# Smaller first loads, earlier loads for the third batch, and closer transposes in a fused attention and rational feed-forward kernel

## Chip, cores and metric

The kernel runs on one core of one Trainium2 chip. The metric is the device time of one execution in microseconds (us). The experiments ran in three jobs, each on one core of a chip of its own (chip 14 for e1 to e4, 6 for e5 to e8, 9 for e9 to e12), and each job also timed the kernel before beside its own kernels; so times are compared within a job, and between jobs only as ratios to the kernel before. For a single core a run counts as slow when it is over 1.5% above the fastest run of the same kernel; one run here was (it is named below), and it is left out of the ratios.

## The reference

Eight batches of attention over 12 heads, 448 tokens and 64 channels per head, with one extra unit in the softmax's denominator; then a feed-forward layer whose activation is a quotient of two polynomials.

```python
scores = scale * q @ k.T                      # batch 8, heads 12, seq 448, head_dim 64
e      = exp(scores - m)
attn   = e / (sum(e) + exp(-m) + 1e-9)
x      = (attn @ v) as [8 * 448, 768]
h      = x @ w_in                             # [768, 2048]
g      = (a0 + a1*h + a2*h^2 + a3*h^3) / (1 + |b0|*|h| + |b1|*h^2 + 1e-6)
out    = g @ w_out                            # [2048, 768], float32
```

## The kernel before

The kernel is a software pipeline over batches. In slot `n` (six slots to a batch) it makes the scores and exponentials of one pair of heads, while the feed-forward layer of the batch before (`gemm1`, product with `w_in`) and of the one before that (`gemm2`, product with `w_out`) fill TensorE. A list of (slot, function) is sorted by slot; TensorE and ScalarE follow that order exactly. VectorE, GpSimd and SyncE are placed by a scheduler, so for them the slot only sets the order in which work is offered.

The loads go out from GpSimd. Batches 0 and 1 have q and k transposed on TensorE (`transpose_pair`); from batch 2 on a DMA transposes them (`transpose_dma`), issued from SyncE.

```python
    def load(b, quads=range(NQ)):
        if quads[0] == 0:
            ...                                   # tiles q4, k4, v4, qT, kT of this batch; zero two margins of q4
        for qd in quads:                          # four heads at a time, 224 KB per tensor
            h0, h1 = 4 * qd, 4 * qd + 4
            nc.gpsimd.dma_start(out=k4[:, h0*w:h1*w]..., in_=runs(k))
            nc.gpsimd.dma_start(out=q4[:, D+h0*w:D+h1*w]..., in_=runs(q))
            nc.gpsimd.dma_start(out=v4[:, h0:h1]..., in_=runs(v))

    def transpose_dma(b):
        nc.sync.dma_start_transpose(out=kT..., in_=k4)                       # kT
        nc.sync.dma_start_transpose(out=qT[:, T:]...[:, :, 0, :], in_=q4[:, D:D + H*NJ*D])
        nc.sync.dma_start_transpose(out=qT[:, 0:2*nb*T]...[:, :, 0, :], in_=q4[:, 0:H*NJ*D])
        nc.sync.dma_start_transpose(out=qT[:, 2*nb*T:]..., in_=q4[:, H*NJ*D:])

    def transpose_pair(b, p):
        g0, g1 = 8 * p + (1 if p else 0), 8 * p + 9      # pair 0: nine blocks of q, the ninth reads head 2
        for i, g in enumerate(range(g0, g1)):
            nc.tensor.transpose(tq[...], q4[:, g * D:(g + 2) * D], ident[0:T, 0:T])
        nc.vector.tensor_copy(out=qT[...], in_=tq[...])
        ...                                              # four blocks of k, the same way, into kT

    load(0, [0])
    ...
    load_w_in(0, 2); load(1, [0]); load_w_in(1, 2); load(1, range(1, NQ))

    for b in range(B):
        if b >= 2:
            work.append((b * NP - NP - 1.5, load, (b,)))
            work.append((b * NP - NP - 1.49, transpose_dma, (b,)))
        for p in range(NP):
            n = b * NP + p
            if b < 2:
                work.append((n - 0.95, transpose_pair, (b, p)))
            ...                                          # scores at n + 0.0 and n + 0.5
        for qd in range(NQ):
            n = b * NP + 2 * qd
            work.append((n + 2.02, sums, (b, qd)))
            work.append((n + 2.52, attend, (b, qd)))
        ...                                              # gemm1, the activation, gemm2
    work.append((2 * NP - NP - 1.4, load_w_out, ()))     # 3 MB in one DMA
```

The softmax here doesn't subtract the row's maximum and nothing guards it: scores larger than these inputs give would overflow.

## Time and profile before

| | |
|---|---|
| time | 470.21 us, median of 3 (469.68 to 471.07) |
| span of the profiled run | 468.7 us |
| TensorE / VectorE / ScalarE busy | 93% / 78% / 65% |

The table of stretches gives busy time per engine in a stretch of time. The columns are: stretch and its length, then busy time and count of instructions of PE (TensorE matmuls), PEld (weight loads), DVE (VectorE), ACT (ScalarE) and POOL (GpSimd), then granted TensorE clock (1.00 is full speed, 0.50 half), mean busy share of the DMA engines, and GB/s. In the lines of this document `sps` are scores, `e` their exponentials, `den` and `rden` the sums and their reciprocals, `u` the product with v, `hp` the product with `w_in`, `op` that with `w_out`; `tq` and `tk` are transposes on TensorE.

```profile
core 0: us, PE busy (x) PEld busy (x) DVE busy (x) ACT busy (x) POOL busy (x), PEclk, DMA share, GB/s
...
70.00:80.00 10.00, 6.00 (x39) 2.15 (x37) 7.84 (x12) 5.92 (x7) 2.40 (x6) 0.79 0.83 137
80.00:90.00 10.00, 10.00 (x76) 4.09 (x73) 7.19 (x12) 8.54 (x9) 9.15 (x15) 0.87 1.37 181
90.00:100.00 10.00, 7.06 (x66) 2.75 (x64) 9.15 (x13) 7.58 (x9) 1.33 (x2) 0.82 1.39 185
...
200.00:300.00 100.00, 99.82 (x771) 48.61 (x770) 87.36 (x126) 69.69 (x73) 9.03 (x17) 1.00 0.55 92
```

From 200 to 300 us TensorE is full at full clock. In the stretches from 70 to 100 us it has holes (times in which TensorE idles), and the clock is down. The list of waits between 60 and 105 us says what for (engine, line, whom it waited for; total us, times, longest):

```profile
PE sps L178 <- DMA qT<-q: 3.7, 1, 3.7
PE sps L178 <- ACT e L183: 3.6, 4, 2.5
```

The chain of waits is followed back from the last instruction. Its early part, in order of time (start, length, what):

```profile
6.04 7.71 DMA k<-in_k_dram
...
14.03 12.95 DMA q<-in_q_dram
...
27.27 11.84 DMA v<-in_v_dram
...
39.40 9.15 DMA k<-in_k_dram
...
48.64 15.27 SPq L100
...
64.02 5.91 SPq L102
...
69.99 7.44 DMA qT<-q
77.43 0.14 issue
77.56 0.99 PE sps L178 x4
```

All that stands before the third batch's scores at 77.56 us is transfers: the loads, and then the DMA transposes, which take 29 us from 48.6 us on. qT comes in three pieces, the last of them short; I call the landing of the second piece (the third of the four DMA transposes), at 77.43 us, the gate. GpSimd's own timeline shows what shares the DMA engines with the transposes (start, length, engine, line, operation, what ended the idle time before it):

```profile
41.80 1.17 POOL L164 DMA_DIRECT2D w_out_sb<-in_moe_w_out_dram  x1 [0.46 <-DMA q<-in_q_dram]
70.32 0.72 POOL L85 DMA_DIRECT2D k<-in_k_dram  x1 [27.36 <-DMA kT<-k]
77.76 0.15 POOL L68 MEMSET q<- 112x64 f16 x1 [6.72 <-DMA qT<-q]
...
79.95 2.10 POOL L90 DMA_DIRECT2D v<-in_v_dram  x3 [0.29 <-issue]
```

`w_out` goes out before the transposes start. The third batch's v goes out after the gate, because GpSimd, which works in order, first waits for qT at a memset.

### The profile page before, as it was taken

To read this page: it belongs to the slowest core of one execution; us is meant where nothing else is said; L and a number is where in the kernel's file an instruction comes from. 1 tells how busy PE (TensorE), PEld (TensorE's weight loads), DVE (VectorE), ACT (ScalarE), POOL (GpSimd) and SP (SyncE) were. 2 spreads that over 40 slices of the span, in tenths; PEclk is the share of its full clock that TensorE was granted. 3 is DMA by queue.
4 is the path that set the end of the run, shared out by engine and by line. 5 is a ranking of instruction groups with operands and counts; after the bars stand their busy time and mean duration, and the time that the engine had idled before them with its cause. 6 is when DMAs were issued, how large, how long until landed. Compare 5 with 4: busy or idle time off the path is not lost.

```text
span 468.7 us, 8030 instructions
## 1 busy us (share of the span) xinstructions
PE 436.7 (93%) x3346; PEld 214.3 (46%) x3346; DVE 364.6 (78%) x536; ACT 307.0 (65%) x331; POOL 76.8 (16%) x133
## 2 busy tenths in 40 slices
PE   2888986979999999999999999999999999999695
PEld 1444432434444454444544444444444445555353
DVE  1234796988999988888989998888989989999800
ACT  2788686667778675659588766658686773566411
POOL 7443003713314001230020001010000000200000
PEclk9999997979999999999999999999999999999989
DMA  9999998999798418991391109811011100110222
GB/s 123 205 205 196 206 169 135 191 180 175 132 167 152 73 31 144 166 149 36 66 184 60 35 0 169 138 34 36 1 34 35 35 23 12 40 48 16 67 69 67
DMA packets 91764, 46.90 MB, mean 100 GB/s; under 512 B 52304, under 2 KB 86608, under 8 KB 91728
## 3 DMA queue, kind: packets, MB, share of 16 engines
q0 software_dynamic: 37136, 22.81, 34.7%
q1 hardware_dynamic: 54592, 23.58, 26.0%
q8 instruction: 26, 0.43, 0.4%
q14 instruction: 10, 0.08, 0.1%
HBM read 45.62 MB, written 11.01 MB: 121 GB/s over the span
## 4 chain that ended last, share of the span: by engine, by line
PE 69%; DMA 10%; DVE 7%; ACT 5%; SPq 5%; issue 1%; POOL 1%; DVEq 0%; POOLq 0%
PE op L322 28%; PE hp L224 24%; PE sps L178 7%; PE u L189 7%; ACT e L183 4%; DMA k<-in_k_dram 4%; PE den L189 4%; SPq L100 3%; DMA q<-in_q_dram 3%; DMA v<-in_v_dram 3%; DMA qT<-q 2%; SPq L102 1%; DVE w L268 1%; DVE g L284 1%; DVE w L273 1%
## 5 line engine op out<-in xcount | busy, mean ns | idle before, releaser
L183 ACT ACTIVATE e<-sps 112x896 f16<-112x896 f32 x192 | 164.6, 915 | 103.8 <-PE sps L178 103.7
L224 PE MATMUL hp<-xt,w_in_sb 128*128 128x448 f16 x768 | 163.4, 357 | 0.6 <-ACT rden L201 0.6
L322 PE MATMUL op<-w_out_sb,g 128*128 128x384 f16 x768 | 133.4, 329 | 3.7 <-DVE g L284 3.7
L224 PEld LDWEIGHTS <-w_in_sb 128*128 128x128 f16 x768 | 68.9, 98 | 84.6 <-issue 31.3
L322 PEld LDWEIGHTS <-g 128*128 128x128 f16 x768 | 75.5, 99 | 57.1 <-DVE g L284 4.4
L232 DVE CAST g<-hp 128x448 f16<-128x448 f32 x112 | 69.1, 619 | 21.0 <-PE hp L224 20.9
L178 PE MATMUL sps<-qT,kT 64*112 64x448 f16 x384 | 64.2, 390 | 15.1 <-ACT e L183 8.7
L279 ACT ACTIVATE c<-c,oneeps_c 128x1792 f16<-128x1792 f16 (+1 forms) x33 | 57.4, 1740 | 14.9 <-DVE c L261 14.9
L283 ACT ACTIVATE c<-c 128x1792 f16<-128x1792 f16 (+1 forms) x33 | 54.5, 1650 | 0.1
L298 POOL COPY gx<-g 128x256 f16<-128x256 f16 x32 | 16.6, 533 | 194.1 <-DVE g L284 131.1
L178 PEld LDWEIGHTS <-kT 64*112 64x112 f16 x384 | 21.1, 129 | 53.0 <-issue 48.5
L284 DVE TENSOR_TENSOR g<-w,c 128x1792 f16<-128x1792 f16 (+1 forms) x33 | 35.5, 1075 | 12.5 <-ACT c L283 12.0
L189 PE MATMUL u<-e,v 112*32 112x448 f16 x768 | 43.0, 368 | 0.0
L261 DVE TENSOR_TENSOR c<-c,w 128x1792 f16<-128x1792 f16 (+1 forms) x33 | 35.1, 1063 | 0.9
L273 DVE TENSOR_TENSOR w<-w,g 128x1792 f16<-128x1792 f16 (+1 forms) x33 | 35.0, 1059 | 0.4
L268 DVE TENSOR_TENSOR w<-w,g 128x1792 f16<-128x1792 f16 (+1 forms) x33 | 34.9, 1056 | 0.4
L213 DVE TENSOR_TENSOR xt<-u,rden 128x448 f16<-128x448 f32 x48 | 29.1, 618 | 6.3 <-PE u L189 6.0
L329 DVE COPY osb<-op 128x384 f32<-128x384 f32 x48 | 26.5, 552 | 5.7 <-PE op L322 5.2
L85 POOL DMA_DIRECT2D k<-in_k_dram x24 | 17.4, 727 | 80.4 <-DMA kT<-k 74.9
L189 PEld LDWEIGHTS <-v 112*32 112x32 f16 x768 | 18.9, 99 | 21.7 <-issue 9.3
L121 DVE COPY qT<-tq 128x896 f16<-128x896 f16 (+1 forms) x12 | 7.6, 632 | 22.9 <-PE tq L119 22.9
L90 POOL DMA_DIRECT2D v<-in_v_dram x24 | 17.5, 732 | 45.0 <-PE u L189 41.8
(37 smaller groups left out, 278.7 us busy)
## 6 DMA issues: line engine op xcount, KB each, us to landing
k<-in_k_dram POOLq DMA_DIRECT2D x24, 224.0 KB, 8.3
q<-in_q_dram POOLq DMA_DIRECT2D x24, 224.0 KB, 7.5
v<-in_v_dram POOLq DMA_DIRECT2D x24, 224.0 KB, 7.4
w_in_sb<-in_moe_w_in_dram POOLq DMA_DIRECT2D x8, 384.0 KB, 12.7
w_out_sb<-in_moe_w_out_dram POOLq DMA_DIRECT2D x1, 3072.0 KB, 26.0
out_dram<-osb SPq DMA_DIRECT2D x8, 336.0 KB, 2.7
out_dram<-osb SPq DMA_DIRECT2D x8, 288.0 KB, 3.1
out_dram<-osb SPq DMA_DIRECT2D x8, 240.0 KB, 2.6
```

The lines of the kernel that those rows point to most:

```text
L178: nc.tensor.matmul(out=sps[0:T, half, 0:S], lhsT=kT[r, (2 * h + i) * T:(2 * h + i + 1) * T], rhs=qT[r, c:c + S], start=True, stop=True,)
L183: nc.scalar.activation(out=e, in_=sps[0:T, :, 0:S], func=AF.Exp, scale=scale)
L189: nc.tensor.matmul(out=dst[32 * t:32 * t + 32, 0:S], lhsT=w(4 * qd + t, j), rhs=ets[b, 4 * qd + t, j // 2][:, j % 2, :], start=(j == 0), s ...
L224: nc.tensor.matmul(out=hp[:, 0:S], lhsT=w_in_sb[:, c, fc * 128:(fc + 1) * 128], rhs=xt[:, c, :], start=(c == 0), stop=(c == NDC - 1),)
L232: nc.vector.tensor_copy(out=h, in_=hp[:, 0:S])
L261: nc.vector.tensor_tensor(out=c, in0=c, in1=ns[b, gi, f0], op=ALU.mult)
L268: nc.vector.tensor_tensor(out=m, in0=m, in1=h, op=ALU.mult)
L273: nc.vector.tensor_tensor(out=m, in0=m, in1=h, op=ALU.mult)
L279: nc.scalar.activation(out=c, in_=c, func=AF.Ln, bias=oneeps_c)
L283: nc.scalar.activation(out=c, in_=c, func=AF.Exp, scale=-1.0)
L284: nc.vector.tensor_tensor(out=gs[b, gi][:, f0:f0 + n, :], in0=ns.pop((b, gi, f0)), in1=c, op=ALU.mult)
L322: nc.tensor.matmul(out=op[:, 0:HD], lhsT=lhs(fc), rhs=w_out_sb[:, fc, nh * HD:(nh + 1) * HD], start=(fc == 0), stop=(fc == NFC - 1),)
```

## The change

Its intent is to start sooner (first loads by two heads, so that the first transposes needn't wait for four), to bring the third batch's q and k in sooner, and to place transposes closer to the scores that need them. The core of the diff:

```diff
-    load(0, [0])
+    load(0, "kq", [0], 0, 2)
+    load(0, "kq", [0], 2, 4)
...
-    for qd in range(1, NQ):
-        load(0, [qd])
+    load(0, "v", [0])
+    load(0, "kqv", range(1, NQ))
...
     load_w_in(0, 2)
-    load(1, [0])
+    load(1, "kq", [0])
     load_w_in(1, 2)
-    load(1, range(1, NQ))
+    load(1, "v", [0])
+    load(1, "kqv", range(1, NQ))
...
         if b >= 2:
-            work.append((b * NP - NP - 1.5, load, (b,)))
-            work.append((b * NP - NP - 1.49, transpose_dma, (b,)))
+            n = b * NP - NP - (3.5 if b == 2 else 1.5)
+            work.append((n, load, (b, "kq")))
+            work.append((n + 0.01, transpose_dma, (b,)))
+            work.append((n + 0.02, load, (b, "v")))
...
-                work.append((n - 0.95, transpose_pair, (b, p)))
+                early = (0.75, 0.6)[b] if n else 1
+                work.append((n - early, transpose_pair, (b, p)))
...
-            work.append((n + 2.52, attend, (b, qd)))
+            work.append((n + (2.52 if b else 2.3), attend, (b, qd)))
...
-    work.append((2 * NP - NP - 1.4, load_w_out, ()))
+    work.append((NP - 3.4, load_w_out, ()))
```

`load` now takes which tensors and which heads of a quad to load; with all of them it issues what it issued before.

More of the change, by code (lines that the diff above doesn't have):

```diff
@@ L62, with tiles_of, load @@
     loaded = {}
-    def load(b, quads=range(NQ)):
-        if quads[0] == 0:
-            q4 = ld.tile([T, D + H * NJ * D + D], F16, tag="q4", name="q4")
-            eng = nc.vector if b == 0 else nc.gpsimd
-            eng.memset(q4[:, 0:D], 0.0)
-            eng.memset(q4[:, D + H * NJ * D:], 0.0)
-            loaded[b] = (
-                q4,
-                ld.tile([T, H * NJ * D], F16, tag="k4", name="k4"),
-                ld.tile([T, H, NJ, D], F16, tag="v4", name="v4", bufs=2),
-                ld.tile([128, (1 + H * NJ) * T], F16, tag="qT", name="qT", bufs=2),
-                ld.tile([128, H * NJ // 2 * T], F16, tag="kT", name="kT", bufs=2),
-            )
+    def tiles_of(b):
+        q4 = ld.tile([T, D + H * NJ * D + D], F16, tag="q4", name="q4")
+        eng = nc.vector if b == 0 else nc.gpsimd
+        eng.memset(q4[:, 0:D], 0.0)
+        eng.memset(q4[:, D + H * NJ * D:], 0.0)
+        loaded[b] = (
+            q4,
+            ld.tile([T, H * NJ * D], F16, tag="k4", name="k4"),
+            ld.tile([T, H, NJ, D], F16, tag="v4", name="v4", bufs=2),
+            ld.tile([128, (1 + H * NJ) * T], F16, tag="qT", name="qT", bufs=2),
+            ld.tile([128, H * NJ // 2 * T], F16, tag="kT", name="kT", bufs=2),
+        )
+    def load(b, what, quads=range(NQ), t0=0, t1=4):
+        if b not in loaded:
+            tiles_of(b)
         q4, k4, v4, _, _ = loaded[b]
@@ L80, in load @@
         for qd in quads:
-            def runs(src):
-                return src[b].rearrange("(t g) (p j) d -> g p t (j d)", g=NQ, j=NJ)[qd]
-            h0, h1 = 4 * qd, 4 * qd + 4
-            nc.gpsimd.dma_start(
-                out=k4[:, h0 * w:h1 * w].rearrange("p (h x) -> p h x", x=w), in_=runs(k))
-            nc.gpsimd.dma_start(
-                out=q4[:, D + h0 * w:D + h1 * w].rearrange("p (h x) -> p h x", x=w),
-                in_=runs(q))
-            nc.gpsimd.dma_start(
-                out=v4[:, h0:h1].rearrange("p h j d -> p h (j d)"), in_=runs(v))
+            h0, h1 = 4 * qd + t0, 4 * qd + t1
+            for one in what:
+                src, dst = {
+                    "k": (k, k4[:, h0 * w:h1 * w].rearrange("p (h x) -> p h x", x=w)),
+                    "q": (q, q4[:, D + h0 * w:D + h1 * w].rearrange(
+                        "p (h x) -> p h x", x=w)),
+                    "v": (v, v4[:, h0:h1].rearrange("p h j d -> p h (j d)")),
+                }[one]
+                nc.gpsimd.dma_start(out=dst, in_=src[b].rearrange(
+                    "(t g) (p j) d -> g p t (j d)", g=NQ, j=NJ)[qd, :, t0:t1])
     def transpose_dma(b):
```

## The prediction

> **What bounds it now.** By the table of stretches, TensorE is busy 99 to 100% at full clock from 110 to 440 us: that work is conserved. Before it there are holes. TensorE waits 7.0 us for the first queries; then scores and exponentials take turns until about 40 us. The weightiest hole is at 73.8 to 77.56 us: the list of waits gives "scores, for the DMA of qT", 3.7 us, and the chain of waits runs back from it through transfers alone to the first load. So the third batch's DMA transposes, landed at 77.43 us, are a gate: what TensorE gains before 74 us only widens the hole. The granted clock falls to 0.50 at about 76 to 83 us, and again at 96 to 103 us, after a 2.5 us hole that waits for ScalarE behind VectorE. (The Trainium skill, "TensorE: Matmul & The Clock Gate", Part 1, gives windows of 3.4 us; both half-clock stretches last 6.8 us, which agrees.)
>
> **What the change does, read from the built order of instructions.**
> 1. First loads by two heads. The first transposes can start about 1.2 us sooner, but the ninth transpose of pair 0 reads head 2, which comes with the second half, at about 7.0 us again. Eight are then done: first scores some 0.7 us sooner (9.11 to about 8.4, an estimate from 0.11 us per cold transpose). The stream of transfers is full either way (about 200 GB/s from 4 to 64 us).
> 2. Transposes later by 0.2 to 0.35 of a slot, first batch's attend sooner: swaps of neighbours, no work added. Up to 2 us sooner before the gate, nothing after it.
> 3. Third batch's loads. GpSimd's order is nearly the old one: the same bytes stand ahead of its q and k, and w_out still follows them. So k lands near 48.5 us and the transposes still share the queues with w_out. The trace's packet records show about 112 packets a microsecond of each while both run, and up to 1000 for transposes alone: alternation by packet, as the Trainium skill says ("DMA: Bandwidth & Descriptors", Queues, rings and completion order). The one real move: the three v loads (224 KB each) issue right behind the fourth batch's first k, near 71 us, not at 80 us after qT has landed. They meet the tail of the qT transposes: some 290 more packets of 60 ns alternate with it on 16 engines, an estimated 1 us later at most, 0.5 us in the middle. v is needed at 97 us and was no wait before.
>
> **On the critical path.** Earlier start of the stream, -0.2 us; contention with v, +0.5 us; half-clock stretches in other windows, -1 us with luck. The gains of 1 and 2 are swallowed by the gate.
>
> **Prediction: 469.6 us, 466.5 to 472.2 us.** Faster by over 2%: 0.03; within 2%: 0.95; slower by over 2%: 0.02.
>
> **What the profile would show.** First scores at about 8.4 us. The hole before the third batch's scores still there and wider (4 to 6 us), ended by the DMA of qT at 76.5 to 79 us. v landed before 85 us. The hole near 94 us of about 2.5 us still there. From 110 us on, the same length within 1 us.
>
> **What would make it wrong.** If qT lands several microseconds sooner, because q and k of batch 2 or w_out are issued sooner than I think, the clock stays full, and 5 to 8 us are to be had. If v takes its full share for all its 3.4 us, the gate moves by 3 us: 473 us or more. If the second half-clock stretch vanishes, 3 us are gained that I don't count on.

## The result

The changed kernel took 470.99 us in the median (470.33 to 471.46, 4 runs); the kernel before, timed beside it, took 470.48 us (469.68 to 471.07, 4 runs). The ratio is 1.0011, with a 95% interval of 0.9991 to 1.0031. Ratios here are the mean time of one kernel's fast runs over that of the other's of the same rounds, so they aren't quite the ratio of the medians. In a later job (run e11) the ratio was 1.0072 (0.9991 to 1.0154). So the change does nothing that can be told from zero.

The profile after, however, is not that of before. The stretches:

```profile
70.00:80.00 10.00, 8.40 (x75) 3.75 (x72) 10.00 (x17) 8.09 (x9) 2.95 (x4) 1.00 1.42 135
80.00:90.00 10.00, 8.46 (x82) 3.59 (x81) 9.73 (x15) 8.59 (x10) 7.72 (x13) 1.00 1.23 153
90.00:100.00 10.00, 7.27 (x68) 3.14 (x69) 9.89 (x15) 7.79 (x10) 2.27 (x4) 0.99 1.39 188
...
200.00:300.00 100.00, 99.82 (x773) 48.70 (x770) 87.40 (x126) 70.16 (x74) 9.50 (x17) 1.00 0.55 92
```

The clock is full where it was down. The same waits between 60 and 105 us:

```profile
PE sps L176 <- ACT e L181: 4.4, 5, 2.2
...
PE sps L176 <- DMA qT<-q: 1.3, 1, 1.3
```

The hole before the third batch's scores shrank from 3.7 to 1.3 us. But the chain shows that the gate did not come sooner; it came 4.0 us later (81.41 us for 77.43 us):

```profile
49.20 15.59 SPq L97
...
64.90 4.65 SPq L99
...
69.60 11.81 DMA qT<-q
81.41 0.14 issue
81.55 0.59 PE sps L176 x4
```

The hole shrank because TensorE itself came later. GpSimd's timeline shows v in its new place, before the wait for qT:

```profile
69.89 0.72 POOL L91 DMA_DIRECT2D k<-in_k_dram  x1 [26.06 <-DMA kT<-k]
70.60 2.35 POOL L91 DMA_DIRECT2D v<-in_v_dram  x3
82.28 0.49 POOL L67 MEMSET q<- 112x64 f16 x1 [9.33 <-DMA qT<-q]
```

Reading four marks off the two traces accounts for the whole result:

| us | before | after | difference |
|---|---|---|---|
| TensorE done with all it may do before the third batch's scores ("arrival") | 73.82 | 80.23 | +6.4 |
| third batch's scores start | 77.56 | 81.55 | +4.0 |
| first product with `w_out` starts | 104.07 | 104.53 | +0.5 |
| from there to the end | 364.6 | 364.6 | 0.0 |

TensorE is 6.4 us later, and the gate is 4.0 us later. From the gate to the first product with `w_out`, before needed 26.5 us, of which 12.0 us were at half clock by the clock records (75.9 to 82.7 us and 96.3 to 103.2 us, counted from the gate on); after needs 23.0 us with 3.4 us at half clock. That is 3.5 us won back. That it goes with the clock is borne out by all 14 profiles: this stretch takes 21.3 to 22.7 us with no half clock in it (five profiles), 23.0 to 24.0 us with 3.4 us of it (four, and 25.1 us in e6, which also waits for v), 25.8 and 26.0 us with 10.2 us, and 26.5 and 27.2 us with 12.0 and 12.6 us. The last row (span minus third row) shows that nothing behind that point matters: it lies between 364.3 and 364.7 us in every profile, so the rest of this document is about the first 105 us.

### The profile page after: what moved, and what is told of

Read it like the earlier page. It is cut to its first block, busy times and chain, and to the rows that moved or that the text cites. A ratio compares the mean times of both kernels' runs of the same rounds, so it can differ in the third digit from the quotient of the medians.

```text
span 469.2 us, 8033 instructions
## 1 busy us (share of the span) xinstructions
PE 436.0 (93%) x3346; PEld 215.1 (46%) x3346; DVE 364.5 (78%) x536; ACT 306.9 (65%) x331; POOL 78.8 (17%) x135
## 4 chain that ended last, share of the span: by engine, by line
PE 68%; DMA 11%; DVE 7%; ACT 5%; SPq 4%; issue 1%; POOL 1%; DVEq 0%; POOLq 0%
PE op L320 28%; PE hp L222 23%; PE sps L176 7%; PE u L187 7%; ACT e L181 4%; DMA k<-in_k_dram 4%; PE den L187 3%; SPq L97 3%; DMA q<-in_q_dram 3%; DMA v<-in_v_dram 3%; DMA qT<-q 3%; SPq L99 1%; DVE w L266 1%; DVE g L282 1%; DVE w L271 1%
## 5 line engine op out<-in xcount | busy, mean ns | idle before, releaser
L327 DVE COPY osb<-op 128x384 f32<-128x384 f32 x48 | 26.5, 552 | 5.7 <-PE op L320 5.5
L252 DVE TENSOR_SCALAR c<-w,babs 128x1792 f16<-128x1792 f16 (+1 forms) x33 | 24.5, 741 | 0.2
```

## The experiments

### What the parts do to the built program

Before any run, each part of the change was built alone. The third batch's part (the slots of its loads and of `w_out`) leaves the instruction lists of all five engines, with their waits, unchanged (but for the numbers in buffers' names): put into the kernel before, it gives the program of before; taken out of the changed kernel, it gives the changed program. The scheduler places these loads by when their buffers come free, and the slot did not decide. What moves the third batch's v ahead of the wait for qT is the placing of the transposes and of the attend together; each alone leaves v behind it. So three parts remain to be run.

Theory A, after reading the traces: the attend, moved in front of the second pair of scores, starves ScalarE and delays TensorE by about 6 us; the early v delays the gate; the two delays meet at the gate, hide each other, and spare the half clock. The rivals: B, the first loads or the transposes cause the late arrival; C, the gate is late for a reason other than v.

The first job ran e1 to e4, five rounds each, sharing 11 runs of the kernel before: median 470.58 us, but from 465.98 to 471.81 us. That scatter is far wider than in the first three runs (469.68 to 471.07), and it limits what times can say; the marks in the profiles are sharper.

### e1: the attend alone

```diff
-            work.append((n + 2.52, attend, (b, qd)))
+            work.append((n + (2.52 if b else 2.3), attend, (b, qd)))
```

> Only the first batch's attend is moved from slot 2.52 to 2.3; the order on VectorE and ScalarE is that of before, and the third batch's v stays behind qT. Theory A (the attend in front of the second pair of scores starves ScalarE): TensorE comes to the third batch's scores 3 to 6 us later than before's 73.8 us, at 77 to 80 us; the hole before them shrinks from 3.7 us to under 1 us; qT still lands at 77 to 78 us; time 466 to 470 us, because the half-clock stretch behind the hole goes too. Rival B (the late arrival in the changed kernel comes from its first loads and from the half-clock stretch they set off): TensorE comes within 1.5 us of 73.8 us, the hole stays over 2.5 us, time as before within 0.7 us.

It took 468.78 us (467.35 to 469.55), ratio 0.9982 (0.9939 to 1.0026). TensorE's timeline at the gate:

```profile
76.47 2.44 PE L220 MATMUL hp<-xt,w_in_sb 128*128 128x448 f16 x12
78.85 0.89 PE L174 MATMUL sps<-qT,kT 64*112 64x448 f16 x4
```

The arrival is at 78.92 us, 5.1 us later than before, qT landed at 76.69 us (a little sooner than expected), and there is no wait and no half clock behind it. Theory A holds and rival B fails as the main cause. Slower before the gate turned out no slower at the end.

### e2: the transposes alone

```diff
-                work.append((n - 0.95, transpose_pair, (b, p)))
+                early = (0.75, 0.6)[b] if n else 1
+                work.append((n - early, transpose_pair, (b, p)))
```

> Only the transposes of the first two batches are placed closer (0.75 and 0.6 instead of 0.95). Theory A: little of the late arrival is theirs; TensorE comes to the gate within 2 us of before's 73.8 us, the hole stays 2 to 5 us, qT lands at 77 to 78 us, time as before within 1 us. Rival (the placement of the transposes is what delays TensorE, since scores then wait for the copies of qT and kT): arrival at 77 us or later, hole under 1 us.

It took 469.84 us (466.03 to 471.02), ratio 1.0000 (0.9951 to 1.0049). The arrival is at 75.82 us, the hole 2.4 us, qT landed at 78.07 us. This is as theory A expected, at its edge: in this one profile the arrival is 2.0 us later, with 6.8 us of half clock before the gate that the first profile of before has not.

### e3: the first loads alone

```diff
-    load(0, "kqv", [0])
+    load(0, "kq", [0], 0, 2)
+    load(0, "kq", [0], 2, 4)
...                                # and batch 1's first v behind the second half of w_in
```

> Only the first loads are cut to two heads and the second batch's first v goes behind the second half of w_in. The first transposes start near 5.8 us, the ninth near 8.2 us, the first scores near 9.6 us instead of 9.1 us (as in the changed kernel). Theory A: that half a microsecond is swallowed by the gate, qT lands at 77 to 78.5 us, the hole is 2.5 to 4 us, time as before within 1 us. Rival B (the first loads set the late arrival of the changed kernel): arrival at 77 us or later.

It took 470.81 us in the median of all six runs (465.54 to 472.98); the ratio is 1.0026 (0.9970 to 1.0082), with the one slow run (472.98 us) left out. Its profile fell on a quick execution (465.54 us): no half clock behind the gate. The ninth transpose of q ran at 7.66 us and the first scores at 9.00 us, not at the expected 9.6 us. The arrival is at 76.85 us, which misses theory A's hole of 2.5 us (1.0 us) and comes close to B's 77 us; this profile has two half-clock stretches before the gate, which the first profile of before has not. So on e3 alone the first loads aren't cleared; e12 decides.

### e4: the changed kernel with v held back

```diff
+    def v_after_qT(b):
+        v4, qT = loaded[b][2:4]
+        x = H * NJ * T - 3
+        nc.gpsimd.tensor_copy(out=v4[:, 0:H:4, 0, 0:2],
+                              in_=qT[0:T, x:x + 2 * NQ].rearrange("p (a c) -> p a c", c=2))
...
+            if b == 2:
+                work.append((n + 0.015, v_after_qT, (b,)))
             work.append((n + 0.02, load, (b, "v")))
```

The copied elements are overwritten by the load; the copy is there only so that the load has to wait for qT.

> The changed kernel with one thing added: the third batch's three v loads wait for its qT, as they did before, through a six-element copy per partition on GpSimd; the orders on TensorE, ScalarE and VectorE are those of the changed kernel. Theory A (v's packets alternate with those of the transposes and delay the gate): qT lands at 77 to 79 us instead of 81.4 us; TensorE, which arrives at about 80.2 us, waits for it no more; time 1 to 2 us under the changed kernel, 469 to 470 us. Rival C (the gate is late because VectorE is busy throughout or the transposes stall by themselves, not because of v): qT lands at 80.5 us or later, time within 0.5 us of the changed kernel's 471.0 us.

It took 469.88 us (468.79 to 470.49), ratio 1.0006 (0.9964 to 1.0049). qT landed at 80.61 us, only 0.8 us sooner than in the changed kernel. On this number rival C wins: v alone is not what made the gate late, and 0.8 us is no more than two executions of one kernel differ by (e8). The time falls where theory A had put it, but it comes from another job than the changed kernel's 470.99 us, and its ratio to before tells nothing.

### e5: the changed kernel with v and the next k held back

This is e4, with the same kind of copy in front of the fourth batch's first k, so that no load at all meets the last two transposes.

> The changed kernel with the third batch's v and the fourth batch's first k both held back until the third batch's qT has landed, so that no load shares the queues with its last two transposes. The orders on TensorE, ScalarE and VectorE stay those of the changed kernel. With v alone held back (e4) qT landed at 80.61 us, against 81.41 us in the changed kernel and 77.43 us before. Theory D (any load whose packets trickle in beside the transposes slows them, and e4 still had one): qT lands at 75 to 78 us, TensorE, arriving near 80.3 us, no longer waits; time as e4, 468.5 to 470.5 us. Rival E (the transposes are late by themselves in this order: the transfers start about 1.1 us later, and a 16 KB instruction fetch near 70.7 us falls into the second transpose): qT lands at 79 us or later all the same.

The second piece of qT landed at 77.28 us (the short third at 78.29 us), and TensorE, arriving at 79.64 us, waited for nothing. In this order theory D holds, E fails. It took 468.94 us (467.39 to 470.24), ratio 0.9966 (0.9928 to 1.0003). So in the changed order the loads beside the transposes cost 4.1 us at the gate (81.41 less 77.28, from two jobs); taking v away first gives back 0.8 us of it, and the rest goes when k is held back too. k alone was not held back. D is no general rule, though: before had the same k beside its transposes and landed at 77.43 us.

Why k costs more in the changed order is open. Two differences between the traces suggest themselves: the stream of loads runs about 1.1 us later (by the packet records it passes 2016 KB at 16.0 us for 14.9 us), and VectorE is busy without a break at 70 to 80 us (10.00 of 10 us, for 7.84 before). Other runs speak against both. e3 has the same k beside its transposes, its loads as late (its first DMA transpose goes out at 49.14 us, that of the changed kernel at 49.20 us), and VectorE busy for the same 10.00 us; its qT landed at 77.75 us. e12 has the late loads (49.34 us) and landed at 78.82 us; e1 has the busy VectorE (10.00 us) and landed at 76.69 us. v landed 11.4 us after its issue in the changed kernel (median), queued behind k and beside the transposes, and 6.2 us before, where VectorE was idle; but it took 5.3 us in e1 and 5.2 us in e4, with VectorE busy throughout. The Trainium skill ("SBUF — State Buffer", the box on DMAs issued from GpSimd under "SBUF: two separate sides") says that VectorE, while it runs an operation in a mode that uses two ports, locks GpSimd out of writing descriptors. In these numbers no such delay shows.

### e6: the kernel before with `w_out` held back

```diff
     def load_w_out():
+        qT = loaded[2][3]
+        x = H * NJ * T - 1
+        nc.gpsimd.tensor_copy(out=w_out_sb[:, 0, 0:2], in_=qT[:, x:x + 2])
         nc.gpsimd.dma_start(out=w_out_sb, in_=...)
```

> The kernel before with w_out held back until the third batch's qT has landed (a two-element copy on GpSimd), so the DMA transposes no longer alternate packet by packet with 3 MB of w_out. Orders on TensorE, ScalarE, VectorE as before. Theory A (that gate is what the early part of the kernel waits for): kT lands by about 55 us and qT by about 65 us; no hole before the third batch's scores, which start at about 74 us; the first product with w_out starts near 95 to 98 us instead of 104 us; time 461 to 465 us, that is 1 to 2% faster than before. Rival F (TensorE is limited by ScalarE and VectorE there, so work bunches up and the time comes back at the later hole near 94 us; or w_out, landing later, becomes the new wait): time within 2 us of before, a longer wait for ScalarE or for w_out behind the gate.

It took 465.01 us (464.40 to 466.55) for 470.84 us: ratio 0.9888 (0.9858 to 0.9919), clear of noise. kT landed at 54.83 us, there was no hole, and the third batch's scores started at 75.00 us. So the gate is what the early part waited for. Two points missed: qT landed at 68.3 us, not by 65 us, with three loads of k beside it, and the first product with `w_out` was at 100.13 us, not by 98 us. Rival F has a share in it: v, now queued behind `w_out`, became a new wait, and the half clock followed (matmuls of u took 3.18 us for 1.70 us).

```profile
92.42 0.40 PE L177 MATMUL sps<-qT,kT 64*112 64x448 f16 x2 [1.96 <-ACT e L182]
93.23 0.40 PE L177 MATMUL sps<-qT,kT 64*112 64x448 f16 x2 [0.41 <-ACT e L182]
94.63 3.18 PE L188 MATMUL u<-e,v 112*32 112x448 f16 x32 [1.00 <-DMA v<-in_v_dram]
```

### e7: the changed kernel with `w_out` held back

The same edit, in the changed kernel.

> The changed kernel with the same hold on w_out. With the gate gone, the changed kernel's slower path to it should show in the time. Theory A: TensorE comes to the third batch's scores at about 80 us and does not wait; first product with w_out at 101 to 103 us; time 466 to 469 us, 4 to 7 us slower than e6. Rival: the changed order's early delay is only the gate's shadow; time within 1.5 us of e6.

It took 469.41 us (469.21 to 472.84), a little over the expected 469 us, ratio 1.0001 (0.9954 to 1.0049), 4.4 us over e6 of the same job. The arrival is at 80.55 us, 5.5 us after e6's, and nothing holds TensorE there. Without the gate, most of the changed order's late arrival reaches the end (4.4 us between the medians; 2.7 us between the two profiled runs, of which e6's has the half clock behind the gate and e7's has not); with the gate it was hidden.

### e8 and e11: both kernels once more

> The kernel before, rebuilt from the changed source with every part undone (its instruction lists are the same, word for word), profiled once more on this chip: how far the marks move from one execution to the next. All theories: qT lands at 77 to 78.5 us, TensorE arrives at 73.5 to 77 us; the half-clock stretches may lie elsewhere, with a time of 466 to 472 us.

The single run took 472.29 us (its state is unknown, being alone). TensorE arrived at 74.73 us, qT landed at 78.61 us, both 0.9 to 1.2 us later than in the first profile, as were the first transposes (7.92 us for 7.04 us); qT and the time fell just outside the expected ranges. The two half-clock stretches were there again, 6.8 us each, and a third of 3.4 us at 29.9 us. So marks move by about 1 us between executions.

> The changed kernel unaltered, on the chip of these runs, because the kernel before scattered from 466 to 472 us in the first job. All theories: first scores at 9.0 to 10.5 us, TensorE at the third batch's scores at 79.5 to 82 us, qT landed at 80 to 83 us, time 470 to 472 us, within 0.5% of before.

It took 471.19 us (471.04 to 473.39); the ratio, 1.0072 (0.9991 to 1.0154), is over the expected 0.5%, with an interval that includes it. First scores at 9.30 us, arrival at 80.67 us, qT at 81.77 us: as in the first profile, within 0.5 us.

### e12: the changed kernel with the attend put back

```diff
-            work.append((n + (2.52 if b else 2.3), attend, (b, qd)))
+            work.append((n + 2.52, attend, (b, qd)))
```

> The changed kernel with the attend of the first batch back at slot 2.52. In the built order this also puts the third batch's v back behind qT. Theory A: TensorE comes to the third batch's scores at 75 to 77.5 us instead of 80.2 us, qT lands at 77 to 79 us instead of 81.4 us, the hole is 1 to 3 us, time 466 to 471 us with the scatter of before. Rival B (the first loads or the placing of the transposes delay TensorE): arrival at 79 us or later.

The arrival is at 74.71 us, qT landed at 78.82 us; time 471.05 us (468.76 to 471.34), ratio 1.0045 (0.9976 to 1.0113).

```profile
72.26 2.44 PE L222 MATMUL hp<-xt,w_in_sb 128*128 128x448 f16 x12
78.95 0.59 PE L176 MATMUL sps<-qT,kT 64*112 64x448 f16 x4 [4.25 <-DMA qT<-q]
79.47 1.13 PE L187 MATMUL den<-e,ones 112*32 112x448 f16 x16
80.53 2.42 PE L222 MATMUL hp<-xt,w_in_sb 128*128 128x448 f16 x6
```

The arrival is 5.5 us sooner than in the changed kernel (a little better than expected), so the attend alone holds most of the 6.4 us, and B is out: the first loads and the transposes are still in this kernel. The hole is 4.25 us, over the expected 3 us, and behind it the matmuls run at half speed: six products with `w_in` take 2.42 us here and 1.31 us in the changed kernel. This is the trade that hides the change: less work held up in front means a longer wait and a colder clock behind.

How the attend does it is seen on ScalarE. Before (the first block of lines) the two exponentials after the sums follow almost at once, and the wait for the attend's matmuls (1.41 us, at 25.85 us) comes behind them; after (the second block), ScalarE waits out the attend's matmuls first, for 2.94 us:

```profile
21.61 0.58 ACT L202 ACTIVATE rden<-rden 128x448 f32<-128x448 f32 x1
22.72 1.72 ACT L183 ACTIVATE e<-sps 112x896 f16<-112x896 f32 x2 [0.54 <-PE sps L178]
```

```profile
22.27 0.58 ACT L200 ACTIVATE rden<-rden 128x448 f32<-128x448 f32 x1
25.79 6.58 ACT L181 ACTIVATE e<-sps 112x896 f16<-112x896 f32 x8 [2.94 <-PE sps L176]
```

There are three attends in the first batch. From about 38 to 45 us the changed kernel also runs at half clock, in both its profiles and in e1, and before does not. The pushes and this half clock together would make up the 5 us; how much is whose was not measured. The half clock alone doesn't: e2, e3 and e10 have 6.8 us of it before the gate too, with the attend in its old place, and arrive at 75.8, 76.9 and 74.8 us, where the changed kernel, e1, e4, e5 and e7, with the same 6.8 us, arrive at 78.9 to 80.7 us.

### e9 and e10: a version that beats both

e9 is the kernel before with `w_out`, the third batch's v and the fourth batch's first k all held back until qT has landed (the edits of e5 and e6). e10 also swaps the very first two loads, q before k.

```diff
-    load(0, "kqv", [0])
+    load(0, "qkv", [0])
```

> The kernel before with w_out, the third batch's v and the fourth batch's first k all held back until the third batch's qT has landed; orders on TensorE, ScalarE and VectorE as before. In e6 v, issued behind w_out, was a new wait of 1.0 us and set off a half-clock stretch, because qT landed only at 68.3 us with three loads of k beside it. Theory D (loads beside the transposes are what slows them): with nothing beside them kT lands by 55 us and qT by 62 us, so w_out and v follow 6 us sooner than in e6, the wait for v goes; time 462 to 465 us, 0 to 2 us under e6. Rival E (the transposes take long by themselves): qT lands at 66 us or later, the wait for v stays.

SyncE's timeline shows each of the large transposes issued in about 3.4 us with nothing beside it:

```profile
48.27 3.42 SPq L97 DMA_TRANSPOSE kT<-k  x1
51.80 3.39 SPq L99 DMA_TRANSPOSE qT<-q  x1
55.24 3.43 SPq L102 DMA_TRANSPOSE qT<-q  x1
58.72 1.22 SPq L106 DMA_TRANSPOSE qT<-q  x1
```

Beside `w_out`, in the kernel before, the first of them took 15.27 us. kT landed at 53.69 us and qT at 60.5 us, as theory D expected, and the wait for v is gone. The time was 464.77 us (463.49 to 466.59) for 468.95 us, ratio 0.9924 (0.9855 to 0.9994).

> e9 with the very first two loads swapped, q before k, so that the nine transposes of q run while k still lands; no further issues. The first transposes start at about 6.3 us instead of 7.0 us, the first scores some 0.5 us sooner, and with the gate gone this reaches the end: 0.3 to 1 us under e9. Rival: the early phase waits for ScalarE anyway, nothing arrives.

e10 took 463.23 us (463.17 to 463.44), ratio 0.9889 (0.9826 to 0.9953). It is quicker than e9 in the same job, by 1.5 us (0.3 to 1 us expected), and its four runs are the closest together. Against before it is no quicker than e6 (0.9888, in another job). The first transposes ran at 5.84 us and the first scores at 8.28 us, for 7.84 and 9.91 us in e9. But its profile reaches the third batch's scores at 74.79 us, e9's at 73.79 us, so the way that I expected the gain to take isn't shown. e10 has no half clock behind its third batch's scores, e9 has 3.4 us; how far the 1.5 us are the swap's and how far the clock's is open.

## Why the prediction was right, and where it was not

The time was predicted at 469.6 us (466.5 to 472.2) and measured at 470.99 us. The sum held; several of its terms didn't, and they cancelled. That the time came out within the range is in part luck: a gate 4.0 us late would alone have put it at 474.5 us, an estimate from the 470.48 us of before.

- **The gate, and the work behind it: right.** "What TensorE gains before 74 us only widens the hole" is borne out in reverse: 5 to 6 us lost in front of the gate cost nothing (e1, and the changed kernel). The gate itself swallowed up to 3.7 us of this, the hole that it had left before; the rest came back behind it, with the clock. Taking the gate away gains 1.1% (e6). From the first product with `w_out` on, both kernels take 364.6 us.
- **Step 1, first scores at about 8.4 us: wrong.** They came at 9.58 and 9.30 us in the two profiles of the changed kernel, and at 9.11 and 9.99 us before. The second half of q was issued at 3.35 to 4.00 us instead of with the first q at 2.09 to 2.70 us, and the ninth transpose waited for it until 8.23 us, not 7.0 us. The step that failed is "the stream of transfers is full either way": in its first microseconds it waits for GpSimd's issues of 0.65 us each (119 and 91 GB/s from 5 to 7 us, for 193 and 165 before). It is still 1.1 us behind at 36 us, and 0.6 us when the DMA transposes start (49.20 us for 48.64 us).
- **Step 2, "up to 2 us sooner before the gate": wrong in sign.** The arrival is 6.4 us later. "Swaps of neighbours, no work added" was true and beside the point: in this phase TensorE and ScalarE take turns, and 32 matmuls of the attend in front of the scores leave ScalarE idle (e1, e12).
- **Step 3: the move of v was seen, its cause and cost were not.** v moved because of step 2's edits; the third batch's part changes nothing in the program. The cost at the gate was put at 0.5 us, with qT at 76.5 to 79 us; the gate came 4.0 us later, at 81.41 us. v's share is 0.8 us (e4); the loads together cost 4.1 us in that order (e5).
- **"Half-clock stretches in other windows, -1 us with luck": mis-sized.** Between the gate and `w_out` 3.5 us came back, with 8.6 us less of half clock. This term saved the prediction. The hole "still there and wider (4 to 6 us)" was wrong, at 1.3 us.
- **v landed before 85 us: right** (81.96 to 83.96 us). **The hole near 94 us: right** (2.2 us).

The Trainium skill's section on the clock ("TensorE: Matmul & The Clock Gate", Part 1) was the key to the size of what a hole costs. The trace agrees on the window: half-clock stretches are 3.4 or 6.8 us long (but for a last one, in the final 4 us of each run).

## What to carry to other kernels

Find the latest transfer that everything must wait for, and read the profile from there. In front of such a gate, gained TensorE time doesn't reach the end, nor does lost time as long as it fits into the wait (3.7 us here), so a change there can show as "same" and still cost most of its delay once the gate is lifted (e7: 4.4 of 5.5 us). To lift it, look at what shares the DMA engines with it: a large load that isn't needed for another 62 us (issued at 41.80 us, first used at 104.07 us), issued just before a chain of DMA transposes, cost 1.1% here (e6). And compare the built orders part by part before reasoning about slots: one third of this change was no change at all.

## What the Trainium skill lacked or had wrong

- "TensorE: Matmul & The Clock Gate" (Part 1, and "HAM oscillation") names idle gaps over about 3.4 us, a whole idle window, as what drops the clock (and, further on, frequent short ones in another kernel). Here single shorter holes were followed by half clock, and not each time: 1.97 us in e9 by 3.4 us of it, 1.96 us in e7 and 1.97 us in e10 by none, 2.5 us before by 6.8 us.
- The same page calls the onset of the full clock variable from run to run, and gives no scatter of whole times. Here the 29 timed runs of the kernel before lay between 464.3 and 471.8 us, and e8's single run took 472.29 us. The clock goes with a part of that: from the gate to the first product with `w_out` before took 26.5 us with 12.0 us of half clock, e10 22.0 us with none. It isn't all: the four runs of e10, at mean granted clocks of 0.987 to 0.992, lay within 0.3 us.
- "DMA: Bandwidth & Descriptors" (Queues, rings and completion order) says that each DMA engine takes turns between queues by packet, but not what it means for transposes beside a load. In the packet records, 256-byte packets of the transposes and 1536-byte packets of `w_out` advanced at 112 each per microsecond; a transpose whose issue took 3.42 us alone (e9) took 15.27 us so.
- "Runtime: NRT & Kernel Launch" (Instruction fetch mechanics) has the DMA fetches of 16 KiB blocks of instructions, but no number for what one does to other transfers. In each of the profiles whose packets I examined, a 16 KB packet of the instruction queue took about 1 us near 64 to 71 us, and some transposes' packets of that time lasted up to 1.3 to 1.5 us. That it stalls them is my reading; no run tested it.
